# Low halves of transposed queries and keys: from behind the weights of a block to ahead of its row maximum

## The chip, the core and the metric

The kernel runs on one core of one Trainium2 chip. That core has five engines that run side by side, each through a queue of its own in the order in which the program issues work: TensorE (PE in the profile; its weight loads are listed as PEld), VectorE (DVE), ScalarE (ACT), GpSimd (POOL) and SyncE (SP, which issues most DMAs). Matmul results land in PSUM, which is split into banks; a bank can take a new result only when everyone has read the old one. The metric is the device time of one execution in microseconds (us); lower is better.

## What is computed

Three layers in a row: an attention with head mixing before and after the softmax, a top-1 mixture of experts, and a dense layer. The change touches the attention alone:

```
# q, k, v: (batch 4, heads 12, sequence 448, head_dim 64)
scores = scale * np.matmul(q, k.transpose(0, 1, 3, 2))
scores = np.einsum('bhij,hg->bgij', scores, w_pre)      # mix the heads
scores = scores - np.max(scores, axis=-1, keepdims=True)
attn = np.exp(scores)
attn = attn / (np.sum(attn, axis=-1, keepdims=True) + 1e-09)
attn = np.einsum('bhij,hg->bgij', attn, w_post)         # mix them again
return np.matmul(attn, v)
...
x = _moe_ref(x=x, **moe_kwargs)     # 8 experts, 1792 tokens, 768 -> 1024 -> 768
return _moe2_ref(x=x, **moe2_kwargs)  # g = h - tanh(h), 768 -> 2048 -> 768
```

## The kernel before

The attention goes through 16 query tiles T (120, 120, 120 and 88 rows for each of the 4 batches). Scores are matmuls in a reduced float32 format; to keep precision, each operand is split into a high part (`kh`, `qh`: the value rounded to that format) and a low part (`kl`, `ql`: what the rounding dropped), and three products are added: high by high, low by high, high by low (`emit_S`).

Queries and keys must be turned (transposed) first. `tr_q(T, half)` turns three head pairs of a query tile on PE, `tr_k(b, p)` one head pair of the keys; both write a PSUM tile (`ptq`, `ptk`) in the bank that the kernel calls "e". Each returns a first closure, which casts the PSUM tile to the high part on ACT (line 287 for `kh`, 304 for `qh`) and itself returns a second closure, which subtracts the high part from the PSUM tile on DVE and so makes the low part (line 288 for `kl`, 305 for `ql`). The bank "e" is free only after that subtraction. There is a single bank "e", and three other kinds of work write to it: the next transpose, the second half of a pair of score matmuls (`emit_S2` computes two head pairs; its second pair goes to the banks "d" and "e"), and the projection `X` (`emit_X`, line 456).

The scores of a tile are copied to SBUF (`ssb`) and re-laid by DMA into 180 blocks of up to 10 rows by 12 heads (`sr`). A hand-written loop over steps s works through the blocks in a software pipeline, with LAG = 2. In step s, in program order:

- loads, then `flush()`: closures left from the last step run, among them the ACT cast to the high part; the DVE subtraction is put on the list `late2`
- `emit_P(s)`: PE mixes the heads of block s (`P`, line 367), DVE takes the negated row maximum (`mx`, line 369)
- `emit_W(s-1)`: three small DVE instructions make the scaled output weights `w` of block s-1 (lines 379, 380, 382)
- `flush2()`: the DVE subtractions on `late2`
- a score matmul group or an attention-times-values group (`AV`), if this step has one
- ACT takes the exponential of block s (`p`, line 372); it needs the maximum
- a conversion of a piece of dense weights, if this step has one (three DVE instructions `ct`, lines 115 to 117, and three on POOL)
- `emit_T(s-2)`: PE multiplies the exponentials of block s-2 with its weights `w`, transposing in the same go (`T`, line 404); ACT copies the result out (`A`, line 409)
- at the end the other PE fillings of the step: `tr_q`, `tr_k`, `emit_X`

So a transpose at the end of step s-1 has its cast and its subtraction in step s. Which step has which filling is set by a table built from `posS`, `posAV` and `at_e`.

Of the kernel before, what the change touches and what calls it, by code (L numbers as in the profile page):

```python
# [30 lines left out]
def body(ctx: ExitStack, tc, q, k, v, w_pre, w_post, emb, tau, w1, w2, win, wout, out):  # L31
# [22 lines left out]
    def ps(tag, nm):  # L54
        if len(PB) > 1:
            tag = {"a": "h", "b": "h"}.get(tag, "o")
        return psum[-1].tile([128, 512], F32, tag=tag, name=nm, bufs=PB[-1][tag])
# [67 lines left out]
    if True:  # L125
# [237 lines left out]
        def emit_P(i):  # L363
            n = 12 * blocks[i][2]
            t = sr.pop(i)
            pt = ps("b", f"P{i}")
            pe.matmul(pt[:n, :S], wpre[:n, :n], t[:n, :], start=True, stop=True)  # L367
            mx = a2.tile([120, 4], F32, tag="mx", name=f"mx{i}", bufs=5)
            dve.tensor_reduce(mx[:n, 0:1], pt[:n, :S], op=ALU.max, axis=AX.X, negate=True)  # L369
            p = a2.tile([120, S], F32, tag="p", name=f"p{i}", bufs=LAG + 1)  # L370
            pj[i] = (p, mx)
            return lambda: act.activation(p[:n, :], pt[:n, :S], AF.Exp, bias=mx[:n, 0:1], scale=1.0, accum_out=mx[:n, 1:2])  # L372
# [3 lines left out]
        def emit_W(i):  # L376
            n = 12 * blocks[i][2]
            p, mx = pj[i]
            dve.tensor_scalar_add(mx[:n, 2:3], mx[:n, 1:2], 1e-9)  # L379
            dve.reciprocal(mx[:n, 3:4], mx[:n, 2:3])  # L380
            w = a2.tile([120, 120], F32, tag="w", name=f"w{i}", bufs=3)
            dve.tensor_scalar_mul(w[:n, :], wpost[:n, :], mx[:n, 3:4])  # L382
            wj[i] = w
# [4 lines left out]
        def emit_T(i):  # L388
            T, r, m = blocks[i]
            n = 12 * m  # L390
            b, it = divmod(T, 4)
            if r == 0:
                A[T] = aA.tile([CP, NJ, H, 120], F32, tag="A", name=f"A{T}", bufs=2)
            p, mx = pj.pop(i)
            w = wj.pop(i)
            wv = w.rearrange("p (g i) -> p g i", i=10)[:n, :, :m]
            pt = ps("c", f"T{i}")
            pv = pt[:CP, :NJ * n].rearrange("p (c g i) -> p c g i", c=NJ, i=m)
            tev[i] = (pt, pv, p, w, wv, n, m)

        def T_mm(i, c0, c1):
            pt, pv, p, w, wv, n, m = tev[i]
            for c in range(c0, c1):
                pe.matmul(pt[:CP, c * n:(c + 1) * n] if m == 10 else pv[:, c], p[:n, c * CP:(c + 1) * CP], w[:n, :] if m == 10 else wv,  # L404
                          start=True, stop=True)

        def emit_TE(i):
            T, r, m = blocks[i]
            act.copy(A[T][:, :, :, 10 * r:10 * r + m], tev.pop(i)[1])  # L409
# [202 lines left out]
    with mctx:  # L612
# [324 lines left out]
        def relay_to(i):  # L937
            while nxt[0] <= min(i, NBK - 1) and blocks[nxt[0]][0] in sdone:
                emit_relay(nxt[0])
                nxt[0] += 1  # L940
# [4 lines left out]
        def flush(tag=None):  # L945
            keep = []
            while late:
                x = late.pop(0)
                if tag in (None, x[0]):
                    y = x[1]()  # L950
                    if x[0] == "e" and callable(y):
                        late2.append((x[0], y))
                else:
                    keep.append(x)
            late.extend(keep)
            if tag:
                flush2(tag)
# [3 lines left out]
        def flush2(tag=None):  # L961
            for x in late2[:]:
                if tag in (None, x[0]):
                    late2.remove(x)
                    x[1]()

        def run_fill(fn, a):
            tag = "d" if fn is emit_AV2 else "e"
            if fn is emit_S2:
                flush("d")  # L970
                flush("e")
            elif fn is not emit_S:
                flush(tag)
            e = fn(*a)
            if fn in (emit_S, emit_S2):
                e()
                if a[1] + (fn is emit_S2) == NP - 1:
                    sdone.add(a[0])
            else:
                late.append((tag, e))  # L980
# [30 lines left out]
        for s in range(NBK + LAG + 6):  # L1011
            todo = side.get(s, [])
            fill = [x for x in todo if x[0] in PEF]
            for fn, a in todo:
                if fn in (load_q, load_k, load_v, conv_load, zero_fill):
                    fn(*a)
            flush()
            relay_to(s + NSR - 1)
            ex = emit_P(s) if s < NBK else lambda: None
            if 0 <= s - 1 < NBK:  # L1020
                emit_W(s - 1)
            flush2()
            for fn, a in todo:
                if fn is emit_R and a[1] in (0, 1, 3):
                    fn(*a)
            i = s - LAG
            on = 0 <= i < NBK
            fill.sort(key=lambda x: x[0] not in (emit_S, emit_S2, emit_AV2))
            if fill and fill[0][0] in (emit_S, emit_S2, emit_AV2):
                run_fill(*fill.pop(0))  # L1030
            ex()
            for fn, a in todo:
                if fn is conv_do:
                    fn(*a)
            if on:
                emit_T(i)
                T_mm(i, 0, NJ)
                flush("d")
                emit_TE(i)
            for x in fill:  # L1040
                run_fill(*x)
            for fn, a in todo:
                if fn in (to_experts, do1) or fn is emit_R and a[1] in (2, 4):
                    fn(*a)
# [334 lines left out]
```

## Time and profile before

| | us |
|---|---|
| median of 3 runs | 1389.68 (1389.34 to 1391.23) |
| the profiled execution | 1395.11 |
| its span, first to last instruction | 1393.4 |
| busy in the span: PE | 1316.0 (94%) |
| PEld | 1145.6 (82%) |
| DVE | 1019.3 (73%) |
| ACT | 741.6 (53%) |
| POOL | 502.2 (36%) |

The rows of the trace stem from the profiled execution. Busy time is the union of an engine's instructions; the span covers all three layers, and the attention's loop takes about the first 535 us of it. Idle time of an engine counts only where that engine sets the pace of its stretch.

### The profile page before, as it was taken

The numbers are of one execution on the slowest core, as the hardware profiler recorded it, in microseconds if no ns is written. First come the engines' busy times: TensorE is split into PE (matmuls) and PEld (weight loads), VectorE is DVE, ScalarE is ACT, GpSimd is POOL, SyncE is SP. The second block draws the span as 40 slices with busy tenths as digits, with TensorE's granted clock in tenths as the row PEclk, the third lists the DMA queues.
The fourth block names the chain that finished last, engine by engine and source line by source line (L and its number), as shares of the span: only waits on it lengthen the run. The fifth ranks groups of instructions, "written<-read, shape, count | busy, mean of one in ns | idle before, by whom it ended". The sixth has DMA issues, their size and how long they took to land. (4 is left out here: it accounts for less than half of the span.)

```text
span 1393.4 us, 24972 instructions
## 1 busy us (share of the span) xinstructions
PE 1316.0 (94%) x9104; PEld 1145.6 (82%) x9104; DVE 1019.3 (73%) x2189; ACT 741.6 (53%) x1518; POOL 502.2 (36%) x495
## 2 busy tenths in 40 slices
PE   8998998999899996999999999789999999999998
PEld 5766766677677775999999998689999889999998
DVE  5776786678667765677776774588888787788886
ACT  6666666666666663454555444464444435544442
POOL 0232332333233314332333331464445344454432
PEclk9999999999999998999999999799999999999999
DMA  6875575566557555777877873422112133212102
GB/s 154 259 245 157 179 207 155 163 188 197 144 166 202 173 152 183 236 235 234 278 248 258 261 233 116 125 68 69 46 46 86 46 99 112 68 47 68 46 24 80
DMA packets 149412, 210.90 MB, mean 151 GB/s; under 512 B 54022, under 2 KB 109494, under 8 KB 149286
## 3 DMA queue, kind: packets, MB, share of 16 engines
q1 hardware_dynamic: 145104, 194.19, 45.4%
q0 software_dynamic: 2640, 12.19, 2.9%
q10 hardware_dynamic: 1542, 2.89, 0.6%
q8 instruction: 73, 1.20, 0.4%
q14 instruction: 53, 0.43, 0.1%
HBM read 135.70 MB, written 35.00 MB: 123 GB/s over the span
## 5 line engine op out<-in xcount | busy, mean ns | idle before, releaser
L120 POOL TENSOR_TENSOR cm<-cm,ct 128x256 f32<-128x256 f32 x96 | 70.2, 731 | 426.5 <-DVE ct L117 394.3
L404 PEld LDWEIGHTS T<-w,p 120*112 120x112 f32 (+1 forms) x1440 | 165.8, 177 | 64.9 <-issue 48.7
L404 PE MATMUL T<-w,p 120*112 120x120 f32 (+1 forms) x1440 | 185.0, 272 | 5.0 <-DVE w L382 3.0
L369 DVE TENSOR_REDUCE mx<-P 120x1 f32<-120x448 f32 x180 | 111.7, 621 | 87.9 <-PE P L367 86.9
L1219 POOL TENSOR_TENSOR gl<-th,gh 128x448 fp32r<-128x448 f32 x64 | 74.9, 1170 | 260.9 <-ACT gh L1218 191.7
L367 PE MATMUL P<-sr,wpre 120*120 120x448 f32 x360 | 166.2, 544 | 1.4 <-ACT p L372 1.4
L372 ACT ACTIVATE p<-P,mx 120x448 f32<-120x448 f32 x180 | 114.0, 633 | 99.6 <-DVE mx L379 87.8
L1270 PE MATMUL o<-woh,gh 128*128 128x384 f32 x448 | 152.8, 341 | 4.9 <-DVE acc L1276 4.9
L1239 ACT ACTIVATE u<-h 128x448 f32<-128x448 f32 x64 | 35.0, 548 | 223.1 <-PE h L1235 223.1
L1272 PE MATMUL o<-woh,gl 128*128 128x384 f32 x448 | 151.1, 337 | 0.0
L1271 PE MATMUL o<-wol,gh 128*128 128x384 f32 x448 | 151.1, 337 | 0.0
L1235 PE MATMUL h<-yh,wil 128*128 128x448 f32 x384 | 143.8, 374 | 3.5 <-POOL wil L1208 3.5
L1233 PE MATMUL h<-yh,wih 128*128 128x448 f32 x384 | 144.0, 375 | 1.2 <-ACT wih L1207 0.6
L1234 PE MATMUL h<-yl,wih 128*128 128x448 f32 x384 | 144.1, 375 | 0.5 <-DVE yl L1182 0.5
L1276 DVE TENSOR_TENSOR acc<-acc,o 128x384 f32<-128x384 f32 x196 | 106.9, 548 | 50.9 <-PE o L1272 50.9
L409 ACT COPY A<-T 112x480 f32<-112x480 f32 x180 | 101.4, 563 | 21.0 <-PE T L404 20.5
L684 PE MATMUL hi<-xhi,w1hi 128*128 128x256 f32 x384 | 108.6, 283 | 0.0
L685 PE MATMUL hi<-xli,w1hi 128*128 128x256 f32 x384 | 108.4, 282 | 0.0
L686 PE MATMUL hi<-xhi,w1li 128*128 128x256 f32 x384 | 108.2, 282 | 0.0
L422 PEld LDWEIGHTS AV<-A,v 112*64 112x64 f32 x1536 | 75.4, 139 | 23.8 <-issue 10.8
L667 PE MATMUL ypi<-w2hi,hhi 128*128 128x384 f32 x272 | 93.1, 342 | 0.1
L668 PE MATMUL ypi<-w2li,hhi 128*128 128x384 f32 x272 | 91.8, 338 | 0.5 <-DVE w2li L637 0.3
(223 smaller groups left out, 3278.1 us busy)
## 6 DMA issues: line engine op xcount, KB each, us to landing
sr<-ssb SPq DMA_DIRECT2D x176, 210.0 KB
r<-in_moe_w SPq DMA_DIRECT2D x72, 384.0 KB
r<-in_moe_w SPq DMA_DIRECT2D x52, 512.0 KB
craw<-in_moe_w_in SPq DMA_DIRECT2D x48, 256.0 KB
craw<-in_moe_w_out SPq DMA_DIRECT2D x48, 256.0 KB
raw<-wi_d SPq DMA_DIRECT2D x15, 768.0 KB
wor<-wo_d SPq DMA_DIRECT2D x15, 768.0 KB
wi_d<-cm SPq DMA_DIRECT2D x48, 128.0 KB
```

Of the source, the lines that this page charges most:

```text
L367: pe.matmul(pt[:n, :S], wpre[:n, :n], t[:n, :], start=True, stop=True)
L369: dve.tensor_reduce(mx[:n, 0:1], pt[:n, :S], op=ALU.max, axis=AX.X, negate=True)
L372: return lambda: act.activation(p[:n, :], pt[:n, :S], AF.Exp, bias=mx[:n, 0:1], scale=1.0, accum_out=mx[:n, 1:2])
L404: pe.matmul(pt[:CP, c * n:(c + 1) * n] if m == 10 else pv[:, c], p[:n, c * CP:(c + 1) * CP], w[:n, :] if m == 10 else wv, start=True, stop ...
L684: pe.matmul(pt[:, :256], wh[:, sl], xh[:, c, :], start=c == 0, stop=False)
L685: pe.matmul(pt[:, :256], wh[:, sl], xl[:, c, :], start=False, stop=False)
L1233: pe.matmul(pt[:, :S], wi[0][:, c, sl], yh[:, c, :], start=c == 0, stop=False)
L1234: pe.matmul(pt[:, :S], wi[0][:, c, sl], yl[:, c, :], start=False, stop=False)
L1235: pe.matmul(pt[:, :S], wi[1][:, c, sl], yh[:, c, :], start=False, stop=c == KD - 1)
L1270: pe.matmul(pt[:, :384], gh[:, sl], wo[0][:, f, n0:n0 + 384], start=f == 0, stop=False)
L1271: pe.matmul(pt[:, :384], gh[:, sl], wo[1][:, f, n0:n0 + 384], start=False, stop=False)
L1272: pe.matmul(pt[:, :384], gl[:, sl], wo[0][:, f, n0:n0 + 384], start=False, stop=f == GF - 1)
```

## The change

The call `flush2()` moves from the loop, where it stood behind `emit_W(s - 1)`, into `emit_P`, between the matmul `P` and the row maximum.

```
@@ emit_P
             t = sr.pop(i)
             pt = ps("b", f"P{i}")
             pe.matmul(pt[:n, :S], wpre[:n, :n], t[:n, :], start=True, stop=True)
+
+            flush2()
             mx = a2.tile([120, 4], F32, tag="mx", name=f"mx{i}", bufs=5)
             dve.tensor_reduce(mx[:n, 0:1], pt[:n, :S], op=ALU.max, axis=AX.X, negate=True)
@@ the loop over steps
             ex = emit_P(s) if s < NBK else lambda: None
             if 0 <= s - 1 < NBK:
                 emit_W(s - 1)
-            flush2()
             for fn, a in todo:
```

The subtractions are the only instructions on `late2`. So DVE's queue alone changes: in each of the 46 steps of the loop that have a subtraction (28 for `ql`, 18 for `kl`), it moves up by four instructions. The queues of PE, ACT, POOL and SP hold the same instructions in the same order as before. In the printed function above, line numbers are those of before; from line 368 on, lines of after stand two further down.

First place: DVE around the step in which the keys' fourth head pair of batch 1 (`kl1_3`) is split, and after which `X0_0` is the next to write bank "e". Before:

```order
L369 TENSOR_REDUCE mx28_1285<-P28_1283 120x1
L379 TENSOR_SCALAR mx27_1229<-mx27_1229 120x1
L380 RECIPROCAL mx27_1229<-mx27_1229 120x1
L382 TENSOR_SCALAR w27_1290<-wpost_125,mx27_1229 120x120
L288 TENSOR_TENSOR kl1_3_1278<-ptk1_3_1272,kh1_3_1277 128x448
L461 TENSOR_REDUCE lg_155<-X0_0_1300 120x8
```

The same place after the change:

```order
L288 TENSOR_TENSOR kl1_3_1278<-ptk1_3_1272,kh1_3_1277 128x448
L371 TENSOR_REDUCE mx28_1286<-P28_1283 120x1
L381 TENSOR_SCALAR mx27_1230<-mx27_1230 120x1
L382 RECIPROCAL mx27_1230<-mx27_1230 120x1
L384 TENSOR_SCALAR w27_1291<-wpost_125,mx27_1230 120x120
L463 TENSOR_REDUCE lg_155<-X0_0_1300 120x8
```

The low part went from behind the weights of block 27 to ahead of the maximum of block 28.

Second place: DVE over two steps in a row that both have a subtraction, first the queries' (`ql8_1`), then the keys' (`kl2_5`). Before:

```order
L369 TENSOR_REDUCE mx79_3248<-P79_3246 120x1
L379 TENSOR_SCALAR mx78_3221<-mx78_3221 120x1
L380 RECIPROCAL mx78_3221<-mx78_3221 120x1
L382 TENSOR_SCALAR w78_3253<-wpost_125,mx78_3221 120x120
L305 TENSOR_TENSOR ql8_1_3240<-ptq8_1_3235,qh8_1_3239 128x360
...
L369 TENSOR_REDUCE mx80_3284<-P80_3282 120x1
L379 TENSOR_SCALAR mx79_3248<-mx79_3248 120x1
L380 RECIPROCAL mx79_3248<-mx79_3248 120x1
L382 TENSOR_SCALAR w79_3289<-wpost_125,mx79_3248 120x120
L288 TENSOR_TENSOR kl2_5_3278<-ptk2_5_3272,kh2_5_3277 128x448
```

After the change (left out in both, at the "...", are the three conversions `ct`, which stay where they were):

```order
L305 TENSOR_TENSOR ql8_1_3240<-ptq8_1_3235,qh8_1_3239 128x360
L371 TENSOR_REDUCE mx79_3249<-P79_3246 120x1
L381 TENSOR_SCALAR mx78_3221<-mx78_3221 120x1
L382 RECIPROCAL mx78_3221<-mx78_3221 120x1
L384 TENSOR_SCALAR w78_3254<-wpost_125,mx78_3221 120x120
...
L288 TENSOR_TENSOR kl2_5_3278<-ptk2_5_3272,kh2_5_3277 128x448
L371 TENSOR_REDUCE mx80_3285<-P80_3282 120x1
L381 TENSOR_SCALAR mx79_3249<-mx79_3249 120x1
L382 RECIPROCAL mx79_3249<-mx79_3249 120x1
L384 TENSOR_SCALAR w79_3290<-wpost_125,mx79_3249 120x120
```

Both low parts now stand first in their step, each ahead of the maximum of its own step's block.

## Rows read from the trace of the kernel before

**Rows 1.** The page: its first line.

```profile
span 1393.4 us, 24972 instructions
```

**Rows 2.** Busy time of PE, PEld, DVE, ACT, POOL (counts); clock, DMA share, GB/s.

```profile
60.00:500.00 440.00, 415.77 (x3608) 306.62 (x3605) 314.20 (x969) 283.40 (x665) 149.59 (x208) 1.00 0.62 181
```

**Rows 3.** Waits of PE, 60 to 500 us: us in total, times, longest us.

```profile
PE S L324 <- DVE kl L288: 8.3, 9, 0.9
PE ptk L281 <- PE T L404: 4.5, 5, 1.0
PE X L456 <- DVE ql L305: 3.9, 4, 1.0
PE X L456 <- DVE kl L288: 3.3, 3, 1.1
PE S L324 <- DVE ql L305: 1.8, 4, 0.7
PE ptk L281 <- issue: 1.7, 1, 1.7
```

**Rows 4.** Groups by line, 60 to 500 us: busy, mean ns, idle before.

```profile
L369 DVE TENSOR_REDUCE mx<-P 120x1 f32<-120x448 f32 (+1 forms) x150 | 93.1, 621 | 71.1 <-PE P L367 70.2
...
L305 DVE TENSOR_TENSOR ql<-ptq,qh 128x360 fp32r<-128x360 f32 (+1 forms) x26 | 12.8, 492 | 0.0
...
L288 DVE TENSOR_TENSOR kl<-ptk,kh 128x448 fp32r<-128x448 f32 x18 | 11.1, 617 | 0.0
```

**Rows 5.** Timeline, first place: start, length in us, [idle before <-releaser].

```profile
91.38 0.53 ACT L287 CAST kh<-ptk 128x448 fp32r<-128x448 f32 x1
...
92.06 0.62 DVE L369 TENSOR_REDUCE mx<-P 120x1 f32<-120x448 f32 x1 [1.09 <-PE P L367]
...
93.23 0.61 DVE L288 TENSOR_TENSOR kl<-ptk,kh 128x448 fp32r<-128x448 f32 x1
...
93.99 0.69 PE L456 MATMUL X<-ien,xT 128*120 128x136 f32 x4 [1.15 <-DVE kl L288]
```

**Rows 6.** Timeline, second place: two steps with a low part each.

```profile
245.18 0.47 ACT L304 CAST qh<-ptq 128x360 fp32r<-128x360 f32 x1
245.28 0.62 DVE L369 TENSOR_REDUCE mx<-P 120x1 f32<-120x448 f32 x1 [0.35 <-PE P L367]
...
246.00 0.64 ACT L372 ACTIVATE p<-P,mx 120x448 f32<-120x448 f32 x1 [0.34 <-DVE mx L379]
...
246.39 0.53 DVE L305 TENSOR_TENSOR ql<-ptq,qh 128x360 fp32r<-128x360 f32 x1
...
246.62 0.56 ACT L409 COPY A<-T 112x480 f32<-112x480 f32 x1
...
247.02 0.57 PE L281 MATMUL ptk<-ident,natk 112*128 112x112 f32 x4 [0.90 <-PE T L404]
...
247.63 0.53 ACT L287 CAST kh<-ptk 128x448 fp32r<-128x448 f32 x1 [0.45 <-PE ptk L281]
...
249.51 0.61 DVE L288 TENSOR_TENSOR kl<-ptk,kh 128x448 fp32r<-128x448 f32 x1
...
250.27 0.43 PE L324 MATMUL S<-kh,qh 64*120 64x448 f32 x1 [0.91 <-DVE kl L288]
```

**Rows 7.** Timeline, such a pair of steps at an 88-row tile.

```profile
78.00 0.38 ACT L304 CAST qh<-ptq 128x264 fp32r<-128x264 f32 x1
...
78.55 0.62 DVE L369 TENSOR_REDUCE mx<-P 120x1 f32<-120x448 f32 x1 [1.80 <-PE P L367]
...
83.54 0.41 PE L324 MATMUL S<-kh,qh 64*88 64x448 f32 x1 [0.94 <-DVE kl L288]
```

**Rows 8.** Timeline, the shortest way from weights to their use.

```profile
203.21 0.28 DVE L382 TENSOR_SCALAR w<-wpost,mx 120x120 f32<-120x120 f32 x1
...
204.87 1.07 PE L404 MATMUL T<-w,p 120*112 120x120 f32 x8
```

More of the change, by code (lines that the diff above doesn't have):

```diff
@@ L367, in emit_P @@
             pe.matmul(pt[:n, :S], wpre[:n, :n], t[:n, :], start=True, stop=True)
+            flush2()
             mx = a2.tile([120, 4], F32, tag="mx", name=f"mx{i}", bufs=5)
@@ L1021, in body @@
                 emit_W(s - 1)
-            flush2()
             for fn, a in todo:
```

## Prediction

> **What bounds the kernel now.** I first took the busy time by stretch. In the attention's steady part, from 60 to 500 us of a span of 1393.4 us [rows 1], PE is busy 415.77 of 440 us, DVE 314.2, ACT 283.4, POOL 149.6, at a granted clock of 1.00 [rows 2]. So PE sets the pace there, and it stands still for 440 − 415.8 = 24.2 us. A change that leaves PE's own instructions alone can take no more than that from this stretch, unless the stretch is not PE's after all.
>
> Next I asked whom PE waits for there. Six kinds of waits make up nearly all of it [rows 3]: score matmuls on `kl` (9 times, 8.3 us), `X` on `ql` (4, 3.9) and on `kl` (3, 3.3), score matmuls on `ql` (4, 1.8), and the key transposes `ptk` (5 times 4.5, put down to the matmul `T` ahead, and once 1.7, put down to issue). The `ptk` rows need a second look, since a matmul does not wait for the one ahead of it on its own engine. In the timeline of such a case `ptk` starts at 247.02, and the query's low part ends at 246.39 + 0.53 = 246.92 [rows 6]: 0.10 us, the same distance as elsewhere between a low part and its waiter (93.23 + 0.61 = 93.84 to 93.99, 0.15 us [rows 5]). What `ptk` waits for is bank "e", which the subtraction holds. All six rows are thus one cause, 26 waits and 8.3 + 4.5 + 3.9 + 3.3 + 1.8 + 1.7 = **23.5 us**: PE needs a low part, or the bank it reads, before DVE has made it.
>
> Third, why is DVE late, with a quarter of its time free? It sits idle 70.2 us before the row maximum, waiting for the matmul `P` [rows 4], and makes the low part only behind that maximum and three more instructions. In the first place the cast is done at 91.38 + 0.53 = 91.91, the maximum begins at 92.06 after an idle time of 1.09 us, and the low part begins at 93.23 [rows 5]: 1.3 us after it could have.
>
> **The change, part by part.** It adds and removes no instruction and issues no DMA; 46 subtractions move up four places in DVE's queue alone, 44 of them in this stretch (26 + 18 [rows 4]). It is told in three parts: what PE gets, what the maximum loses, and where the two meet.
>
> *Steps where one low part is followed by a user of the bank or of the data* (7 waits of `X`, 3 of the 9 on `kl` that are not preceded by a `ptk` wait, 4 on `ql`). First place: with the low part first, it starts as soon as the cast is done, about 91.95 (a DVE instruction starts 0.04 us after its releaser when DVE is idle, as the maximum does after `P`), ends 0.61 later at 92.56, and frees the bank at 92.71. PE was ready for `X` at 93.99 − 1.15 = 92.84 [rows 5]. So this wait goes in full, with 0.13 us to spare. I worked through the other thirteen in the same way and found the same: what is waited for is ready before PE comes. Gain: 3.9 + 3.3 + 1.8 + 3 × 0.92 = **11.8 us** (0.92 is 8.3 / 9).
>
> *Pairs of steps*, a query's low part and in the next step a key's, then score matmuls: 6 pairs with 12 waits, 4.5 + 1.7 + 6 × 0.92 = 11.7 us. Here the moved instruction costs something. In the second place the cast `qh` ends at 245.65; the low part takes 245.69 to 246.22; the maximum, which had run from 245.28 to 245.90, now ends about 246.77, 0.87 later (DVE instructions start 0.08 before the one ahead ends). The exponential follows 0.10 after it, at 246.87 in place of 246.00, the copy of `T` 0.62 after the exponential's start, at 247.49 to 248.05, and only then can ACT cast `kh`: about 248.00 to 248.53, not 247.63. Low part `kl` 248.57 to 249.18, bank free 0.15 later at 249.33: the score matmul starts 0.94 us earlier than its 250.27, of 0.90 + 0.91 = 1.81 us that this pair waits now [rows 6]. So about half of it stays. At an 88-row tile, as in three of the six, `P` is the later of the two: the cast ends at 78.38, the maximum starts at 78.55; the low part (0.42 us there) delays it by only 0.21 [rows 7], and by the same chain the score matmul comes at 81.96 in place of 83.54, 1.58 of 1.90. The three of the first kind wait 6.3 us in all, at 0.94 / 1.81 that gives 3.3; the others 5.5 us, at 1.58 / 1.90 that gives 4.6. Gain: **7.9 us**; 3.8 us stay.
>
> *The other 18 low parts* are waited for by nobody now. Nothing is gained, and the maximum comes later by what the low part sticks out of the idle time, 0.2 to 0.9 us by the two cases above.
>
> *What becomes late.* Behind the low part in DVE's queue stand the maximum of s, the weights of s-1 and the conversion. Their users are the exponential of s on ACT, the matmul `T` of s-1 on PE, and POOL. POOL is busy a third of the time [rows 2] and off the path. `T` is the one that can hurt: in the 44 steps, the shortest distance from the end of the weights to the `T` that reads them is 204.87 − (203.21 + 0.28) = 1.38 us [rows 8], since a step always lies between them. Lateness of 0.2 to 0.9 and PE's own coming 0.43 us earlier at that place leave it at or above 0.05 us even at the worst. So I put this part at 0, with the bound as a rival below.
>
> *Sum*: 11.8 + 7.9 = 19.7 us less PE idle. PE runs without gaps else, so the loop's end, and all that follows it in the program's order, comes 19.7 us sooner: the profiled execution 1395.1 − 19.7 = 1375.4 us. The median of the runs shown lies 5.4 us under the profiled execution; I take the same step from it: 1389.7 − 19.7 = **1370.0 us**, 1.4% faster. Bounds: all 23.5 us go (1366.2), or the pairs give nothing and 11.8 us go (1377.9).
>
> **The rivals.**
>
> *All of it goes* (1366.2 or a little below). For it: PE coming sooner also brings the next transpose sooner. Against it: in the pairs the cast waits for ACT's copy, not for PE.
>
> *Half of it goes.* The wait moves on: after `X` comes a step whose score matmuls want bank "e" back, which needs ACT's copy of `X`, and ACT is now behind by the delay of its exponential. If each wait of `X` came back there and the pairs gave nothing, 23.5 − 7.2 − 11.7 = 4.6 us would be gained, 1385; with half of either, some 12 us, 1378. Against it: in the first place I find about 0.3 us of room there.
>
> *Slower.* DVE works in order, so in each of the 46 steps the maximum now waits for ACT's cast, and with it the exponential, the copy and the next cast: ACT and DVE become a ring. If the shift of 0.87 us at the second place hit PE in all 46 steps, 40 us would be lost against 19.7 gained: 1389.7 + 20 = 1410. Half of that is about the break-even: 46 × 0.43 = 19.8. It decides where the weights come later than the 1.38 us of [rows 8]; then PE waits at `T` for `w`. The Trainium skill's PSUM — Partial Sum Buffer page (section Engine vs sequencer instructions) says that the queues of ScalarE, VectorE and GpSimd are strictly first in, first out; by that rule a low part without its cast holds up the maximum even when `P` is done, and the row agrees in that no instruction of DVE starts ahead of an earlier one in the timelines read. Against this rival speaks that PE now waits for neither `w` nor `p` in this stretch.
>
> *No change.* The bank's users wait for the cast and not for the subtraction, or the 20 us are waited out where the experts begin. Against it: in the first place the cast ends 0.93 us before PE is ready (92.84 − 91.91).
>
> **How the numbers follow.** Likeliest, 15 to 22 us gained: 0.55. All gone (22 to 25): 0.17. About half (8 to 15): 0.14. Little to nothing, up to 8 us gained: 0.06, of which 0.04 lies within 0.2% (2.8 us, about what a measurement of this kernel can tell from no change). Slower: 0.08, of which 0.01 lies within 0.2%. The range from 1365 (24.7 gained) to 1381 (8.7) holds the first three cases, 0.86. Faster by over 0.2%: 0.86 + 0.02 = 0.88; within: 0.04 + 0.01 = 0.05; slower: 0.07.
>
> **What would show it.** In the changed kernel's trace, PE's waits on `kl`, `ql` and of `ptk` in the loop should shrink from 23.5 us to about 4, what is left of them at the six pairs; DVE's idle time before the maximum should fall, with part of it now ahead of the low parts, put down to ACT's casts; PE's busy time should stay. No wait of `T` for `w` or `p` should appear; if it does, the rival of the ring is at work. If PE's waits vanish and the time doesn't move, the loss must show as idle PE where the experts start.

## The result and the profile after

The changed kernel takes 1371.59 us (median of 4 runs, 1370.08 to 1376.32) against 1390.45 us of the kernel before beside it: a ratio of 0.987, 95% interval 0.9843 to 0.9896. That is 1.3% faster, 18.9 us by the medians. The profiled execution took 1376.32 us, 18.8 us less than that of before.

Busy time by stretch, changed kernel, 60 to 500 us, columns as in [rows 2]:

```profile
60.00:500.00 440.00, 435.18 (x3787) 323.42 (x3786) 323.18 (x1015) 293.47 (x702) 149.55 (x208) 1.00 0.65 189
```

PE is now busy 435.2 of 440 us, where it was 415.8. It does no other work: it gets through 3787 matmuls in the time that 3608 took. Over the same work, from the first matmul `P` of block 20 to that of block 179 ("the loop" below, the same matmuls in every kernel here), its idle time falls from 462.24 − 435.54 = 26.7 us to 440.04 − 432.75 = 7.3 us and its busy time by 2.8 us. The prediction had the busy time staying; the section on the hardware says where most of these 2.8 us come from. What PE still waits for, changed kernel, 60 to 500 us (us in total, times, longest):

```profile
PE S L324 <- DVE kl L288: 2.7, 6, 0.5
PE T L406 <- ACT A L411: 1.4, 3, 0.5
PE M L533 <- DVE p L525: 0.2, 1, 0.2
PE ptk L281 <- DVE ql L305: 0.2, 1, 0.2
```

Of the 23.5 us of [rows 3], 2.7 + 0.2 = 2.9 us are left. All seven waits of `X` are gone, and so are the four of score matmuls on `ql`. The page now also puts the `ptk` wait down to `ql`, as the prediction read it. The wait of `T` for the copy `A` is new. DVE's three groups, changed kernel, same stretch (busy, mean ns, idle before):

```profile
L371 DVE TENSOR_REDUCE mx<-P 120x1 f32<-120x448 f32 x160 | 99.0, 619 | 42.5 <-PE P L367 41.9
...
L305 DVE TENSOR_TENSOR ql<-ptq,qh 128x360 fp32r<-128x360 f32 (+1 forms) x26 | 13.0, 500 | 17.4 <-ACT qh L304 17.1
...
L288 DVE TENSOR_TENSOR kl<-ptk,kh 128x448 fp32r<-128x448 f32 x18 | 11.2, 625 | 15.5 <-ACT kh L287 15.3
```

DVE's idle time before the maximum fell from 70.2 us [rows 4] to 41.9, and 17.1 + 15.3 = 32.4 us now stand ahead of the low parts, put down to ACT's casts: the low part fills a hole that DVE had anyway. The first place in the timeline of the changed kernel:

```profile
91.23 0.53 ACT L287 CAST kh<-ptk 128x448 fp32r<-128x448 f32 x1
...
91.80 0.62 DVE L288 TENSOR_TENSOR kl<-ptk,kh 128x448 fp32r<-128x448 f32 x1 [0.57 <-ACT kh L287]
92.34 0.61 DVE L371 TENSOR_REDUCE mx<-P 120x1 f32<-120x448 f32 x1
92.53 0.90 PE L458 MATMUL X<-ien,xT 128*120 128x136 f32 x6
```

From the cast's end, 91.76, to the low part it is 0.04 us, as worked out; it was 1.32 [rows 5]. The bank is read out at 92.42, and `X` starts at 92.53 without a wait. The second place, a pair of steps, changed kernel:

```profile
234.69 0.46 ACT L304 CAST qh<-ptq 128x360 fp32r<-128x360 f32 x1
235.18 0.53 DVE L305 TENSOR_TENSOR ql<-ptq,qh 128x360 fp32r<-128x360 f32 x1 [0.67 <-ACT qh L304]
235.63 0.61 DVE L371 TENSOR_REDUCE mx<-P 120x1 f32<-120x448 f32 x1
235.77 0.60 PE L281 MATMUL ptk<-ident,natk 112*128 112x112 f32 x4
...
236.34 0.63 ACT L374 ACTIVATE p<-P,mx 120x448 f32<-120x448 f32 x1 [1.19 <-DVE mx L381]
...
236.97 0.57 ACT L411 COPY A<-T 112x480 f32<-112x480 f32 x1
...
237.06 0.47 PE L324 MATMUL S<-kh,qh 64*120 64x448 f32 x2
...
237.41 0.54 ACT L287 CAST kh<-ptk 128x448 fp32r<-128x448 f32 x1
...
237.78 0.36 PE L324 MATMUL S<-kh,qh 64*120 64x448 f32 x1
...
237.99 0.62 DVE L288 TENSOR_TENSOR kl<-ptk,kh 128x448 fp32r<-128x448 f32 x1
...
238.67 0.46 PE L324 MATMUL S<-kh,qh 64*120 64x448 f32 x1 [0.53 <-DVE kl L288]
...
239.47 1.07 PE L406 MATMUL T<-w,p 120*112 120x120 f32 x8
```

The `ptk` wait is gone. The score matmul waits 0.53 us in place of 0.91 [rows 6], at the end of the chain that the prediction named: low part, late maximum, exponential, copy, cast, low part. The exponential starts 1.19 us after the end of the query's cast (1.22 worked out), the key's cast 1.07 us after the exponential (1.13 worked out).

### The profile page after: what moved, and what is told of

Same layout as the page of the kernel before. It is cut to its first block, busy times and chain, and to the rows that moved or that the text cites. A ratio compares the mean times of both kernels' runs of the same rounds, so it can differ in the third digit from the quotient of the medians.

```text
span 1374.6 us, 24956 instructions
## 1 busy us (share of the span) xinstructions
PE 1312.8 (96%) x9104; PEld 1146.0 (83%) x9104; DVE 1017.7 (74%) x2189; ACT 736.7 (54%) x1518; POOL 502.8 (37%) x495
## 5 line engine op out<-in xcount | busy, mean ns | idle before, releaser
L424 PEld LDWEIGHTS AV<-A,v 112*64 112x64 f32 x1536 | 74.8, 138 | 23.9 <-issue 10.5
```

## Experiments

Each kernel ran beside the kernel before on the same chip, and its ratio is to that one. Differences between two experiments are taken as the difference of their ratios times 1392 us, since they did not all run on one chip. Where the loop tells more than the whole time, it is given as well; it is from one profiled execution each, 462.2 us before, and 440.0 and 440.2 us in the two profiles of the changed kernel. First the changed kernel once more:

> The changed kernel once more, beside the next three on the same chip: 1371 to 1372 us.

Measured: 1373.25 us, a little above what was expected, ratio 0.9863 (0.9847 to 0.988). This is what the others are set against below. Its traced waits are those of the first profile to 0.1 us.

**Only the keys' low parts, only the queries'.**

```
@@ in emit_P, behind the matmul P
+            flush2(kind=tr_k)     # in the other kernel: kind=tr_q
@@ the loop: flush2() behind emit_W(s - 1) stays, for the rest
```

> Only the 18 low parts of the keys go ahead of the maximum; those of the queries stay behind the weights. Theory (PE waits for the low part or for the bank that it holds): the waits on kl go, 8.3 us of score matmuls and 3.3 us of X, and the waits on ql stay (X 3.9, scores 1.8, and 6.2 us of ptk): PE's waits for low parts fall from 23.5 to about 12 us, the time from 1390.4 to about 1379. Rival (a late maximum costs time, and the move gains elsewhere): the time does not follow the sum of the waits, and waits of T for w or p appear.

> Only the 28 low parts of the queries go ahead of the maximum; those of the keys stay behind the weights. Theory: X's 3.9, the scores' 1.8 and the 6.2 us of ptk go; in the six pairs PE then comes sooner to score matmuls whose key low part comes sooner by less, so part returns there as a longer wait on kl (13 to 15 us in place of 11.6). Net 8 to 10 us less PE idle, about 1381. The gains of this run and of the one with the keys alone add up to about the 19 us of the whole change. Rival (a late maximum costs time): less than 5 us gained, since most low parts are of this kind and PE waits for w or p instead.

Keys alone: 1376.17 us, ratio 0.9888 (0.987 to 0.9905), 16 us gained. Queries alone: 1385.06 us, ratio 0.9952 (0.9937 to 0.9967), 7 us gained. PE's waits with the keys alone moved, 60 to 500 us:

```profile
PE ptk L281 <- issue: 4.9, 4, 1.7
PE X L457 <- DVE ql L305: 3.9, 4, 1.0
PE ptk L281 <- PE T L405: 1.5, 2, 0.8
PE S L324 <- DVE ql L305: 1.3, 3, 0.7
```

and with the queries alone:

```profile
PE S L324 <- DVE kl L288: 10.5, 9, 2.0
PE X L457 <- DVE kl L288: 3.3, 3, 1.1
PE T L405 <- ACT A L410: 1.4, 3, 0.6
PE ptk L281 <- DVE ql L305: 0.5, 3, 0.2
```

Each half takes away its own waits and, but for one short wait of a score matmul on `ql`, no others, as the theory says: 4.9 + 3.9 + 1.5 + 1.3 = 11.6 us stay with the keys alone (about 12 expected), and 10.5 + 3.3 = 13.8 us on `kl` with the queries alone (13 to 15 expected). The new wait of `T` for the copy `A` belongs to the queries' half. The times miss the sums, though: the keys gain 16 us by 12 us of waits, the queries 7 where 8 to 10 were expected, and the two halves make 23 us where the whole makes 19 (in the loop 15.5 + 8.5 = 24.0 where the whole makes 22). The section on the hardware has the reason for the first. For the last, the pairs are the likely reason: with the keys alone no score matmul waits for `kl`, while in the whole change six still do, 2.7 us, since the queries' half makes the keys' cast late again.

**Behind the maximum, ahead of the weights.**

```
-            if 0 <= s - 1 < NBK:
-                emit_W(s - 1)
             flush2()
+            if 0 <= s - 1 < NBK:
+                emit_W(s - 1)
```

> All 46 low parts go behind the maximum but ahead of the three instructions for the weights, so the maximum is not late at all, and the low part comes 0.6 us earlier than before in place of 1.2. Theory: each of the 26 waits shrinks by at most about 0.63 us (the smaller ones go in full): some 15 us gained, about 7 us of waits stay, 1375 to 1376, slower than the whole change by about 4. Rival (the late maximum costs time in the changed kernel): as fast as the whole change or faster, 1371 or below.

Measured: 1377.4 us, ratio 0.9884 (0.9867 to 0.9902), 3 us slower than the whole change by the ratios; 8.9 us of waits stay (3.4 of scores, 3.2 of `X`, 2.3 of `ptk`; the profile puts them down to line 379, the instruction behind the low part, and to `T`). That is the theory's side: a low part that comes only half as much earlier loses more than a maximum in time saves. The intervals of the two touch, but in the loop, too, this kernel is slower, by 6.9 us.

**Another bank for `X`, DVE as before.**

```
-            pt = ps("e", f"X{T}_{hf}")
+            pt = ps("d", f"X{T}_{hf}")
@@ run_fill
-            tag = "d" if fn is emit_AV2 else "e"
+            tag = "d" if fn in (emit_AV2, emit_X) else "e"
```

> DVE's order is that of before; the projection X writes bank d in place of bank e. Theory (X waits for the bank, not for data): its 7 waits of 7.2 us go without any move on DVE, the other waits on low parts (16.3 us) stay; 1383, or up to 3 us above that if AV, which also uses bank d, now waits for X to be read out. Rival (what counts is DVE's order): no gain.

Measured: 1388.31 us, ratio 0.9965 (0.9952 to 0.9978). PE's waits:

```profile
PE S L324 <- DVE kl L288: 8.4, 9, 0.9
PE ptk L281 <- PE T L404: 4.4, 5, 0.9
PE AV L422 <- DVE lg L461: 2.1, 7, 0.3
PE ptk L281 <- issue: 1.7, 1, 1.7
PE S L324 <- DVE ql L305: 1.3, 3, 0.7
```

With DVE's order untouched, the seven waits of `X` are gone, and `AV` waits seven times, 2.1 us, for bank "d". 7.2 − 2.1 = 5.1 us, of which 4 to 5 show in the time. So `X` waited for the bank that the subtraction holds, not for what it computes.

**How late may the maximum be?** A reduction over the block's input is added (into a cell that is overwritten, so the output stays), always in 45 or 46 steps:

```
+            low = bool(late2)     # a low part is about to be made
             flush2()
             mx = a2.tile(...)
+            if low:
+                dve.tensor_reduce(mx[:n, 0:1], t[:n, :], op=ALU.max, axis=AX.X)
             dve.tensor_reduce(mx[:n, 0:1], pt[:n, :S], op=ALU.max, axis=AX.X, negate=True)
```

In the second kernel it reads 64 columns, in the third it stands behind `emit_W`, in the fourth it stands as here but in every third step without a low part.

> The changed kernel with one more reduction over a block's input (its result is overwritten, the output is the same) between low part and maximum in the 46 steps that have a low part: the maximum comes about 0.6 us later still, the low part and the bank do not. Theory (the lateness of the maximum is free but for the six pairs, where it goes by the exponential and the copy to the next cast): 3 to 5 us slower than the changed kernel, as longer waits of the score matmuls on kl, with perhaps some tenths of T waiting for w. Rival (DVE and ACT form a ring that paces the step): 46 times 0.6 us, about 28 us slower, as waits of T for w or p.

> The changed kernel with an extra reduction over 64 columns in place of 448 ahead of the maximum in the 46 steps with a low part, about 0.15 to 0.2 us. Theory (the changed kernel stands just short of the point from which the maximum's lateness is paid): 2 to 6 us slower, about a quarter to a third of the 20 us of the long one or less. Rival (each late maximum costs a fixed amount however late): 10 us slower or more.

> The changed kernel with the same extra reduction of 0.61 us in the same 46 steps, but behind the weights, so that DVE has as much more to do while the maximum and the low part come when they did; its result is overwritten. Theory (what cost 20 us was the lateness of the maximum in these very steps): under 6 us slower than the changed kernel, 1373 to 1379. Rival (DVE has no room left in these steps, whatever stands where): 15 us slower or more, 1387.

> The changed kernel with the extra reduction ahead of the maximum in 45 steps that have no low part (every third of them). Theory (the maximum has room in a plain step, which the low part has used up in the other steps): under 6 us slower, 1373 to 1379. Rival (a late maximum costs its lateness in any step): 15 us slower or more.

| the added reduction | in the trace, each | time, us | ratio to before | slower than the changed kernel | the same, loop alone |
|---|---|---|---|---|---|
| ahead of the maximum, steps with a low part | 0.61 us | 1393.34 | 1.0009 (0.9997 to 1.0022) | 20 us | 22.6 us |
| the same, 64 columns | 0.21 us | 1379.47 | 0.9902 (0.9887 to 0.9918) | 5 us | 9.0 us |
| behind the weights, same steps | 0.61 us | 1378.31 | 0.9888 (0.9869 to 0.9907) | 3.5 us | 6.8 us |
| ahead of the maximum, plain steps | 0.61 us | 1377.28 | 0.989 (0.9875 to 0.9905) | 4 us | 8.0 us |

The first row is a plain miss: 3 to 5 us were expected, and 20 of 46 × 0.61 = 28 us are paid. The intervals of the last two rows overlap that of the changed kernel. PE's longest waits in the first row's kernel:

```profile
PE S L324 <- DVE kl L288: 7.6, 6, 1.3
PE T L409 <- ACT A L414: 3.2, 4, 1.3
PE S L324 <- DVE lg L466: 2.7, 7, 0.4
PE T L409 <- DVE w L387: 2.1, 5, 0.6
PE X L461 <- DVE kl L288: 2.1, 3, 0.9
PE AV L427 <- ACT ssb L328: 1.9, 3, 0.7
```

The lateness comes out in many places. Only 2.1 us of it is `T` waiting for the weights, the place that the prediction watched. A place that it had only among its rivals ("half of it goes", 0.14) is `S` waiting for `lg`, all seven times behind an `X`; the timeline of that kernel shows the way there:

```profile
96.36 0.64 ACT L377 ACTIVATE p<-P,mx 120x448 f32<-120x448 f32 x1 [2.01 <-DVE mx L384]
...
96.99 0.56 ACT L414 COPY A<-T 112x480 f32<-112x480 f32 x1
...
97.44 0.48 ACT L465 COPY raw<-X 120x384 f32<-120x384 f32 x1
...
97.95 0.18 DVE L466 TENSOR_REDUCE lg<-X 120x8 f32<-120x24 f32 x1 [1.11 <-ACT raw L465]
...
98.19 0.44 PE L324 MATMUL S<-kh,qh 64*88 64x448 f32 x1 [0.44 <-DVE lg L466]
```

The same place in the changed kernel:

```profile
93.05 0.63 ACT L374 ACTIVATE p<-P,mx 120x448 f32<-120x448 f32 x1 [1.28 <-DVE mx L381]
...
94.63 0.18 DVE L463 TENSOR_REDUCE lg<-X 120x8 f32<-120x24 f32 x1 [1.01 <-ACT raw L462]
...
94.80 0.51 PE L324 MATMUL S<-kh,qh 64*88 64x448 f32 x2
```

ACT stands idle for 2.01 us before the exponential, where it was 1.28; the copies follow the exponential without a gap, DVE reads `X` after ACT has, and bank "e" is late for the second pair of score matmuls. In the changed kernel DVE has read `X` at 94.63 + 0.18 = 94.81, and that pair starts at 94.80: the waiting has not begun, but there is no room left, where the prediction had found about 0.3 us. The last two rows of the table bear on the cause: the same DVE time behind the weights, or the same lateness in plain steps, costs about a fifth of it by the ratios and about a third in the loop. So most of what is paid is the maximum's lateness in the steps with a low part, though the other two are not free either. The changed kernel has little of that room left: 0.21 us each, 10 us in all, cost 5 us by the ratios and 9 in the loop.

**What is left at the pairs.**

```
@@ first kernel, in emit_P: not in steps that end with a key transpose
-            flush2()
+            if not any(fn is tr_k for fn, _ in side.get(i, [])):
+                flush2()
@@ the loop
+            flush2()
             if 0 <= s - 1 < NBK:
                 emit_W(s - 1)
@@ second kernel, the loop: ex() goes behind emit_TE(i) in the pairs' first steps
```

> The changed kernel, except that in steps which end with a key transpose the low part goes behind the maximum, ahead of the weights. Theory: in the six pairs the maximum is then on time, the key's cast comes up to 0.9 us sooner, and the 2.7 us that score matmuls still wait on kl fall to under 1; ptk may wait 0.1 to 0.4 us more in three of the pairs. 1 to 2 us faster than the changed kernel, 1370. Rival (what is left is due to the cast waiting for PE): no change.

> The changed kernel, except that in the pairs' first steps ACT copies the result of T out ahead of the exponential. Theory: the next cast then waits for the late exponential alone and not for the copy behind it, or not even that; 0.3 to 0.5 us per pair, up to 2 us in all, 1370. Rival: the exponential comes later for it, and T or P two steps on wait for it: no change or some us slower.

The first: 1368.46 us, ratio 0.9835 (0.9817 to 0.9853), 4 us faster than the changed kernel by the ratios, though the intervals touch, and 2.1 us in the loop. In its trace no wait of a score matmul for `kl` is listed any more, but `ptk` waits again, five times and up to 0.7 us, where 0.1 to 0.4 us in three of the pairs were expected; PE's two longest waits, 60 to 500 us:

```profile
PE ptk L281 <- PE T L407: 1.8, 5, 0.7
PE T L407 <- ACT A L412: 1.7, 4, 0.5
```

The pair, now with the query's low part behind the maximum:

```profile
233.87 0.62 DVE L372 TENSOR_REDUCE mx<-P 120x1 f32<-120x448 f32 x1
...
233.93 0.47 ACT L304 CAST qh<-ptq 128x360 fp32r<-128x360 f32 x1
...
234.43 0.53 DVE L305 TENSOR_TENSOR ql<-ptq,qh 128x360 fp32r<-128x360 f32 x1
234.59 0.64 ACT L375 ACTIVATE p<-P,mx 120x448 f32<-120x448 f32 x1 [0.20 <-DVE mx L372]
...
235.06 0.57 PE L281 MATMUL ptk<-ident,natk 112*128 112x112 f32 x4
...
235.67 0.53 ACT L287 CAST kh<-ptk 128x448 fp32r<-128x448 f32 x1
```

The exponential starts 0.10 us after the maximum's end and well before the low part is done, so the key's cast is not held up by it: it starts 0.04 us after `ptk` ends, 1.27 us after the query's ended at 234.40, against 237.41 − 235.15 = 2.26 in the changed kernel. The second, with the copy ahead of the exponential: 1373.74 us, ratio 0.9868 (0.9851 to 0.9884), no change (in the loop 3.4 us slower); `kl` waits of 2.2 us stay and `X` waits 1.2 us again. It was the wrong link to cut.

**Low parts early only where someone waits.** The kernel of the pairs, with the low parts that nobody waits for put back behind the weights (in `emit_P`, `flush2()` only if the step goes on to `X` or scores).

> Low parts stand where somebody waits for them: ahead of the maximum if the step goes on to X or score matmuls and has no key transpose, behind the maximum and ahead of the weights if it ends with a key transpose, and behind the weights, as before the change, in all other steps. Theory: no wait comes back, and fewer maxima are late: as fast as the version with the pairs behind the maximum (1368.5), or up to 2 us faster, 1367 to 1369. Rival: the low parts that nobody waits for are better early too: 2 us slower than that version or more.

Measured: 1369.01 us, ratio 0.9831 (0.9817 to 0.9846): as the version before, within the interval (in the loop 438.7 us against 438.0). Two things cancel there: `T` no longer waits for the copy `A` (1.7 us in the version before), and three score matmuls wait for `ql` again, 1.3 us, though no wait should have come back. So some of the low parts put back are waited for, in a later step. What those that nobody waits for cost by themselves is not shown; in sum it makes no difference where this group stands.

## Why the prediction was right, and where it was off

Forecast were 1370.0 us and a gain of 19.7; measured 1371.6 and 18.9. The mechanism was right; that the two gains agree to 1 us is in part luck, as the last point shows.

- *PE sets the pace, and one cause makes nearly all its idle time*: shown. 23.5 us of waits became 2.9, and the time followed. That `ptk` waits for the subtraction and not for `T` is shown by the run with the keys alone, where these waits stay, and the one with the queries alone, where they go.
- *The steps with one low part, 11.8 us, gone in full*: shown; no such wait is left.
- *The pairs, 3.8 us stay*: 2.9 stayed. The split was off: the three pairs at 120-row tiles keep 1.6 us of score waits where 3.0 were forecast, the three at 88-row tiles 1.1 where it was 0.9. The chain through exponential, copy and cast is shown, by its times at the second place and by the version that takes the low part out of it.
- *What becomes late costs nothing*: held for this change but for 1.4 us, `T` waiting for the copy `A` three times, which was not foreseen. The reason given for it did not hold. The 1.38 us of [rows 8] is not the room that decides: with 0.61 us more in each step with a low part, `T` waits for weights only 2.1 us, while the other five rows shown for that kernel add up to 17.5 us, where the changed kernel has 2.7 + 1.4 = 4.1. At the one place followed in its timeline it is ACT's copies behind the late exponential that pass the lateness on, the way that the rival "half of it goes" had named; for the other rows that is my reading. The rival of the ring was the right mechanism with the wrong place, and it stood much nearer than 0.07 says: 0.61 us more lateness gave the whole gain back.
- *The sum, and that it carries through to the end*: here two misses cancel. From the first matmul `P` of block 20 to that of block 179 the timelines show 462.2 us before (67.07 to 529.31) and 440.0 after (68.68 to 508.72), 22.2 us less, which is more than the forecast: 19.4 us of idle time and 2.8 us of busy time, a term that the prediction put at nothing. Of these 22.2 us, 18.8 are left in the profiled execution. Some 2 us are missing at the end of the experts: from their first to their last matmul into the hidden layer it is 271.4 us before and 273.5 after. In the second profile of the changed kernel the same stretch takes 269.9, and over all the traces 269.1 to 273.8, so that part is scatter. Why the medians, too, show some 3 us less than the loop is open.

## What to carry to other kernels

When a wait names an instruction of an engine that has idle time, look at what stands ahead of it in that engine's queue; moving a ready instruction ahead of one that waits is nearly free as long as it fits into the wait. What does not fit makes the next instruction late, and that is to be followed along every engine behind it, not only to the nearest reader: lengthen it on purpose by some tenths of a microsecond and see what is paid. Where two such steps follow each other, the order that is best for one can be wrong for the pair.

## What the runs showed of the hardware

A wait inside a group of score matmuls costs more than the row says. The six matmuls of a head pair (two heads, each on 64 of the rows, two starting close together) took 237.78 − 237.06 = 0.72 us unbroken at the second place of the changed kernel. The next six, with the wait of 0.53 us between the first head's start and the second's, took 239.47 − 237.78 = 1.69, so 1.16 without the wait: 0.44 us more. The same holds for the whole loop of the kernel before: of its 78 groups, 65 are unbroken and take 0.68 to 0.72 us, the nine that wait for `kl` take 1.11 to 1.14 without the wait, and the four that wait for `ql` 0.92 to 0.97. Beyond the waits listed, the nine thus cost 3.7 us and the four 0.9. With the keys alone moved, PE's busy time in the loop falls from 435.54 to 431.85 us, by 3.7 (with the whole change, which leaves six such waits, by 2.8): that is most of the difference between the 12 us of waits that this took away and the 16 us that it gained. A part of it stands in the rows: the first two matmuls of an unbroken group take 0.47 us together, those of the broken one 0.36 and 0.46, one behind the other. That the lack of overlap between the two heads is all of it is my reading.
